# A delta-rule attention with a feed-forward: opening stage ordered by hand, weight decoding spread over VectorE, ACT and POOL beside the first feed-forwards, joins placed later

## The chip, the cores and the metric

The kernel runs on one core of a Trainium2 chip. The engines are TensorE (PE in the profile, PEld for its weight loads), VectorE (DVE), ScalarE (ACT), GpSimd (POOL) and SyncE (SP, which issues transfers). In these traces each of them works through its own instructions in the order as built, and one that has to wait holds up everything behind it: in the changed kernel VectorE stands 4.0 us behind one step of POOL, and a long transpose some steps further on starts at 175.9 us; without that kind of POOL step (run e2) it starts at 171.3.

## The reference, cut to what matters

```python
# attention: B=4, H=8, S=768, D=48; per head a 48 x 48 state
k_n = k / (norm(k, axis=-1) + 1e-6)
for t in range(S):
    y[t]  = q[t] @ state
    v_old = state^T k_n[t]
    state = state + beta[t] * outer(k_n[t], v[t] - v_old)
# feed-forward on x = y as (3072, 384); w_in 384 x 2048, w_out 2048 x 384, float64
out = gelu_exact(x @ w_in) @ w_out
```

Inputs are fp32 except the two weights. These arrive as 64-bit floats, which no step of the kernel reads as such: the kernel takes the two 32-bit words of each number and rebuilds an fp32 from mantissa, exponent and sign ("decoding").

## The kernel before

The sequence is cut into 12 chunks of 64 positions. For each pair of chunks (a "group") the loop over positions becomes a triangular system. Its parts are:

- *grams*: products of K and Q of a chunk (psG), packed into the tile `diag`;
- *flip*: VectorE transposes `diag` to `Nu`, so that all 32-row blocks are solved side by side;
- *elimination*: 30 pairs of dependent VectorE steps (`tmp`, then `Nu`), then three transposes back (`XM`, and `Zf` twice): the inverse;
- *joins*: TensorE joins the 32-row inverses to 64-row ones (psJ);
- *state steps*, chunk by chunk, because each needs the state of the one before: psK, W, psU, U, psY, x, psS, St, and psX/xT, x transposed for the feed-forward;
- *feed-forward* of a chunk: 16 times fc1 (psH) with a Gelu on ACT, then fc2 (psO).

Nothing of a feed-forward can start before the weights it needs are decoded, and nothing of chunk c's feed-forward before x of chunk c. The weights come in parts, each decoded by five VectorE steps and two POOL steps between them:

```python
def decode(n):
    ...
    nc.vector.tensor_scalar(e, hi, 20, 0x7FF, shift_right, and)          # exponent
    nc.vector.tensor_scalar(bits, hi, 0xFFFFF, 0x100000, and, or)        # high mantissa
    nc.gpsimd.tensor_scalar(e, e, 1151.0, 896.0, min, max)
    nc.gpsimd.tensor_scalar(e, e, -896.0, 2**23, add, mult)
    nc.vector.scalar_tensor_tensor(e, hi, 0x80000000, e, and, or)        # sign
    nc.vector.scalar_tensor_tensor(dst, lo, 2.0**-32, bits, mult, add)   # low mantissa
    nc.vector.scalar_tensor_tensor(dst, dst, 2.0**-20, e, mult, mult)
```

The order of the program is made by `interleave`, which spreads lists of steps over each other in proportion (a scheduler then still moves instructions within each engine):

```python
interleave(gram_steps(0) + gram_steps(1) + v_steps(0) + inverse_steps(0),
           [(1.0, decode, n) for n in range(6)])
interleave(state_steps(0), gram_steps(2) + v_steps(1),
           [(1.0, decode, n) for n in range(6, n_in)])
for c in range(1, NC):
    more = gram_steps(c + 2) + v_steps(c + 1) + (inverse_steps(c // 2 + 1) if c % 2 else [])
    ...  # c == 1: also the decode of w_out
    interleave(state_steps(c), more, ffn_steps(c - 1))
```

The norms of K take a power of one half on POOL (`nc.gpsimd.tensor_tensor(flat, flat, half, op=ALU.pow)`).

## Time and profile before

The kernel before took 827.5 us (median of 3 runs, 825.4 to 828.5). Its milestones, read from the timeline:

| milestone of the kernel before | us |
|---|---|
| first flip starts | 31.2 |
| first inverse (XM) ready | 102.0 |
| first fc1 | 126.5 |
| first feed-forward over | 213.0 |
| second feed-forward over | 267.6 |
| span | 825.5 |

How to read it: from 267.6 us on TensorE is busy for all but 14 of 558 us. Before that it is not, and what it waits for is VectorE.

### The profile page before, as it was taken

What the parts mean: (1) busy time and instruction counts of PE and PEld (TensorE: products, weight loads), DVE (VectorE), ACT (ScalarE), POOL (GpSimd) and SP (SyncE); (2) the same over time, 40 slices, a digit from 0 to 9 for tenths busy, and PEclk for the clock granted to TensorE, in tenths of its full rate; (3) what the DMA queues carried; (4) which work ended last, traced back from release to release, by engine and by line L of the source; (5) the groups of instructions that cost most, each with busy time, mean ns of one, the idle gap of its engine ahead of it and who ended that gap; (6) DMA issues with size and microseconds to landing.
All of it is one profiled execution on the core that took longest, in us unless ns stands there. A gap on an engine that the chain in (4) does not pass through costs nothing.

```text
span 825.5 us, 18581 instructions
## 1 busy us (share of the span) xinstructions
PE 707.5 (86%) x8148; PEld 515.3 (62%) x8148; DVE 376.1 (46%) x874; ACT 220.4 (27%) x510; POOL 190.9 (23%) x178
## 2 busy tenths in 40 slices
PE   4111078967999999999989999989999999999997
PEld 4100066735776865866857867757768668677684
DVE  3597997896012594031791023971125931202000
ACT  4200054201331512332403324213325122021120
POOL 8735357413002303013202014012023000000000
PEclk8555558887899999999999999999999999999999
DMA  7266034401101201203101102011011000000000
GB/s 173 111 154 107 19 90 106 102 33 30 35 16 29 50 1 30 40 12 61 19 20 31 30 21 54 6 30 31 2 30 30 2 21 2 10 11 1 20 1 19
DMA packets 84784, 32.85 MB, mean 40 GB/s; under 512 B 78048, under 2 KB 81120, under 8 KB 84704
## 3 DMA queue, kind: packets, MB, share of 16 engines
q1 hardware_dynamic: 80064, 26.75, 14.7%
q10 hardware_dynamic: 4640, 4.92, 2.4%
q8 instruction: 64, 1.05, 0.5%
q14 instruction: 16, 0.13, 0.0%
HBM read 26.94 MB, written 4.72 MB: 38 GB/s over the span
## 4 chain that ended last, share of the span: by engine, by line
PE 67%; DVE 20%; POOL 5%; issue 3%; SPq 2%; ACT 1%; DMA 1%; POOLq 0%; DVEq 0%
PE psO L460 28%; PE psH L451 25%; DVE tmp L283 4%; DVE Nu L285 4%; POOL w_e L187 2%; DVE w_e L189 2%; PE psT L235 2%; PE psS L426 2%; PE psG L248 2%; SPq L89 2%; PE psK L365 2%; PE psJ L320 1%; PE psJ L323 1%; DVE U L391 1%; PE psU L385 1%
## 5 line engine op out<-in xcount | busy, mean ns | idle before, releaser
L451 PE MATMUL psH<-xT,w_in_sb 128*128 128x256 f32 x1152 | 273.8, 390 | 4.0 <-ACT g L454 3.3
L460 PE MATMUL psO<-w_out_sb,g 128*128 128x384 f32 x768 | 273.6, 506 | 0.0
L451 PEld LDWEIGHTS psH<-xT,w_in_sb 128*128 128x128 f32 x1152 | 214.6, 192 | 36.4 <-ACT g L454 3.7
L460 PEld LDWEIGHTS psO<-w_out_sb,g 128*128 128x128 f32 x768 | 143.8, 194 | 91.0 <-issue 7.3
L454 ACT ACTIVATE g<-psH 128x256 f32<-128x256 f32 x192 | 73.7, 384 | 180.5 <-PE psH L451 179.9
L391 DVE TENSOR_TENSOR U<-psU,gm 64x192 f32<-64x192 f32 x88 | 31.2, 354 | 108.4 <-PE psU L385 107.5
L283 DVE TENSOR_TENSOR tmp<-Nu 128x30 f32<-128x30 f32 (+9 forms) x180 | 63.2, 351 | 4.6
L285 DVE TENSOR_TENSOR Nu<-Nu,tmp 128x30 f32<-128x30 f32 (+9 forms) x180 | 63.3, 352 | 4.4
L263 POOL TENSOR_TENSOR P<-G,mask 128x512 f32<-128x512 f32 x24 | 35.4, 1477 | 103.9 <-ACT G L253 103.9
L464 ACT COPY o_sb<-psO 128x384 f32<-128x384 f32 x24 | 11.5, 479 | 152.4 <-PE psO L460 152.4
L320 PE MATMUL psJ<-XM,off 32*32 32x32 f32 x768 | 16.4, 203 | 40.3 <-DVE XM L294 40.3
L235 PE MATMUL psT<-ident,Kp 128*128 128x128 f32 x96 | 17.0, 307 | 39.1 <-DMA Kp<-in_k_dram 29.1
L418 DVE TENSOR_TENSOR x<-psY,y 64x192 f32<-64x192 f32 x88 | 31.0, 352 | 38.4 <-PE psY L410 24.4
L320 PEld LDWEIGHTS psJ<-XM,off 32*32 32x32 f32 x768 | 15.2, 119 | 46.7 <-issue 43.4
L301 POOL MEMSET Zf<- 32x1024 f32 x12 | 11.4, 954 | 140.4 <-DVE Zf L298 140.1
L213 POOL TENSOR_TENSOR ksq<-Kp 128x384 f32<-128x384 f32 x24 | 20.7, 864 | 90.3 <-DMA Kp<-in_k_dram 90.0
L375 DVE TENSOR_TENSOR W<-psK,V 128x384 f32<-128x384 f32 x22 | 12.3, 557 | 61.9 <-PE psK L365 61.6
L187 POOL TENSOR_SCALAR w_e<-w_e 128x384 uint32<-128x384 uint32 (+1 forms) x28 | 27.4, 977 | 55.2 <-DVE w_e L183 54.9
L329 ACT COPY XM<-psJ 32x512 f32<-32x512 f32 x24 | 13.9, 578 | 97.7 <-PE psJ L320 97.6
L235 PEld LDWEIGHTS psT<-ident,Kp 128*128 128x128 f32 x96 | 12.7, 157 | 41.9 <-issue 35.9
L236 ACT COPY KQt<-psT 128x512 f32<-128x512 f32 x48 | 26.7, 588 | 43.6 <-PE psT L235 39.5
L214 DVE TENSOR_REDUCE n<-ksq 128x8 f32<-128x384 f32 x24 | 13.2, 552 | 55.2 <-POOL ksq L213 55.2
(75 smaller groups left out, 669.9 us busy)
## 6 DMA issues: line engine op xcount, KB each, us to landing
w_out_sb<-in_moe_w_in_dram SPq DMA_DIRECT2D x12, 512.0 KB, 4.7
w_raw<-in_moe_w_out_dram SPq DMA_DIRECT2D x16, 384.0 KB, 3.3
Kp<-in_k_dram SPq DMA_DIRECT2D x48, 96.0 KB, 2.9
Qp<-in_q_dram SPq DMA_DIRECT2D x48, 96.0 KB, 3.0
V<-in_v_dram SPq DMA_DIRECT2D x48, 96.0 KB, 2.9
out_dram<-o_sb ACTq DMA_DIRECT2D x48, 96.0 KB, 2.2
w_in_sb<-in_beta_dram ACTq DMA_DIRECT2D x2, 96.0 KB, 3.4
```

What stands on the lines that cost most here:

```text
L187: nc.gpsimd.tensor_scalar(e, e, 1151.0, 896.0, op0=ALU.min, op1=ALU.max)
L235: nc.tensor.transpose(psT[:, j, :], flat[:, j * 128:(j + 1) * 128], ident)
L236: nc.scalar.copy(u.KQt[:, :, :, x, :], psT.rearrange("q j (p n) -> q j p n", p=2))
L263: nc.gpsimd.tensor_tensor(u.P, G[:, :, C:], mask_h, op=ALU.mult)
L283: nc.vector.tensor_tensor(tmp, nu[:, j + 1:, j:j + 1].to_broadcast([128, n, j]), nu[:, j:j + 1, 0:j].to_broadcast([128, n, j]), op=ALU.mult)
L285: nc.vector.tensor_tensor(nu[:, j + 1:, 0:j], nu[:, j + 1:, 0:j], tmp, op=ALU.add)
L320: nc.tensor.matmul(psJ[low, 0, col], lhsT=off[top, u, :], rhs=xm[top, u, :], start=True, stop=True)
L391: nc.vector.tensor_tensor(pairs(u.U[HALF[p]], s), pairs(psU[HALF[p ^ s], p], s), pairs(gv[HALF[p]], s), op=ALU.mult)
L418: nc.vector.tensor_tensor(dst, src, pairs(u.y[HALF[p ^ s]], s), op=ALU.add)
L451: nc.tensor.matmul(psH, lhsT=w_in_sb[:, m, f * 128:(f + 1) * 128], rhs=xTs[c][:, m, :], start=(m == 0), stop=(m == NM - 1))
L454: nc.scalar.activation(gs[f], psH, ACT.Gelu)
L460: nc.tensor.matmul(u.psO, lhsT=gs[f][:, u.a * 128:(u.a + 1) * 128], rhs=w_out_sb[:, f, :], start=(f == 0), stop=(f == NF - 1))
```

## The change

The intent has five parts. (1) The opening is ordered by hand, free of most decode, with its own faster ways for square root and packing. (2) Only five half-width parts of the weights are decoded in the opening; 25 full parts go beside the first feed-forward, with the last steps of the small ones. (3) The decode drops from five VectorE steps to four; ACT takes two, POOL keeps one, the last product. (4) Everything after the opening is placed on a time line (`at(first, last, steps)`, in units of feed-forwards), with the joins behind the next chunk's first fc1. (5) K gets more tiles, so that it can be loaded earlier. The core of the diff, with cuts:

```diff
+        nc.vector.tensor_scalar(bits, hi, 0xFFFFF, 0x100000, op0=ALU.bitwise_and, op1=ALU.bitwise_or)
+        nc.scalar.mul(dst, bits, 2.0 ** -20)
         nc.vector.tensor_scalar(e, hi, 20, 0x7FF, op0=ALU.logical_shift_right, op1=ALU.bitwise_and)
-        nc.gpsimd.tensor_scalar(e, e, 1151.0, 896.0, op0=ALU.min, op1=ALU.max)
-        nc.gpsimd.tensor_scalar(e, e, -896.0, float(2 ** 23), op0=ALU.add, op1=ALU.mult)
+        nc.scalar.activation(e, e, ACT.Relu, bias=lim[:, 0:1], scale=float(2 ** 23))
+    def signed(n):
+        nc.vector.scalar_tensor_tensor(dst, lo, 2.0 ** -52, dst, ALU.mult, ALU.add)
         nc.vector.scalar_tensor_tensor(e, hi, 0x80000000, e, ALU.bitwise_and, ALU.bitwise_or)
-        nc.vector.scalar_tensor_tensor(dst, lo, 2.0 ** -32, bits, ALU.mult, ALU.add)
-        nc.vector.scalar_tensor_tensor(dst, dst, 2.0 ** -20, e.bitcast(F32), ALU.mult, ALU.mult)
+        nc.gpsimd.tensor_tensor(dst, dst, e.bitcast(F32), op=ALU.mult)
 ...
+    by_hand.enter_context(tc.manual_schedule(...))      # opening: grams, flip, elimination,
+    for fn, *args in rows:                              # joins of chunk 0, decode(0..4),
+        fn(*args)                                       # state of chunk 0, joins of chunk 1
 ...
+    plan = [at(c + 1, c + 2, ffn_steps(c)) for c in range(NC)]
+    plan += [at(1.0, 1.6, rest), ...]                   # rest: the other decode steps
+    plan += [..., at(1.6, 1.75, gram_steps(3)), at(1.75, 2.45, eliminate_steps(1)),
+             at(2.5, 2.62, join_steps(1)), at(2.62, 2.97, state_steps(2)), ...]
+    for w in range(3, NC):
+        plan += [at(w + 0.25, w + 0.95, state_steps(w))]
+        if w % 2:
+            plan += [at(w - 0.16, w - 0.15, [(1.0, prep, w + 2)]),
+                     at(w, w + 0.2, gram_steps(w + 2)),
+                     at(w + 0.2, w + 0.95, eliminate_steps(w // 2 + 1)),
+                     at(w + 1.02, w + 1.2, join_steps(w // 2 + 1))]
```

In the changed kernel the lines of the decode steps are L195, L197 (ACT), L198, L200 (ACT), L205, L206 and L207 (POOL's product); L252 is POOL's power, L333 the flip, L341 and L343 the elimination, L352 and L356 the transposes back, L378 and L381 the joins.

## The prediction

> **What bounds the kernel now.** I read the page's busy shares first, then the slices, then the busy-time windows cut at the feed-forwards' beginnings, then the timeline, tile and wait views of the stretches that stood out. The slices show two kernels in one:
>
> ```profile
> PE   4111078967999999999989999989999999999997
> DVE  3597997896012594031791023971125931202000
> PEclk8555558887899999999999999999999999999999
> ```
>
> TensorE is nearly idle for six slices of 20.6 us, half used for four more, then full. VectorE is the reverse. The cuts for the next view are the first fc1 matmul (126.5 us), the end of the first feed-forward (213.0) and of the second (267.6). Columns: stretch, length, busy us of PE, PEld, DVE, ACT, POOL, then granted clock.
>
> ```profile
> 0.00:126.50 126.50, 37.57 (x729) 31.48 (x729) 94.65 (x200) 29.82 (x62) 72.17 (x82) 0.56 0.46 110
> 126.50:213.00 86.50, 71.33 (x803) 50.30 (x800) 66.36 (x151) 20.07 (x45) 32.57 (x32) 0.83 0.24 60
> 213.00:267.60 54.60, 54.60 (x584) 39.71 (x577) 9.86 (x24) 16.91 (x40) 7.92 (x7) 1.00 0.15 30
> 267.60:825.50 557.90, 543.98 (x6048) 393.79 (x6046) 205.22 (x500) 153.63 (x364) 78.21 (x59) 0.99 0.11 22
> ```
>
> The last 558 us are TensorE-bound with 14 us of idle time; no rearrangement gains more than that there. The prize is the first 213 us, in which TensorE worked 109 us, much of it at half clock. The timeline says what it waited for: one VectorE chain from the first flip (L275) to the transposed-back inverse (L294), against the same chain for a later group, where no weights are decoded (in brackets: idle time before, and its releaser).
>
> ```profile
> 31.17 1.92 DVE L275 STREAM_TRANSPOSE Nu<-diag 128x1024 f32<-128x1024 f32 x1 [0.86 <-ACT diag L259]
> ...
> 100.01 2.00 DVE L294 STREAM_TRANSPOSE XM<-Nu 128x1024 f32<-128x1024 f32 x1
> ...
> 279.35 1.98 DVE L275 STREAM_TRANSPOSE Nu<-diag 128x1024 f32<-128x1024 f32 x1 [0.51 <-ACT diag L259]
> ...
> 308.02 2.08 DVE L294 STREAM_TRANSPOSE XM<-Nu 128x1024 f32<-128x1024 f32 x1
> ```
>
> The first takes 70.8 us, the later one 30.7 us, of which 2.9 are two interleaved U groups: 27.8 us alone. So 43 us of the opening is weight decoding threaded into the elimination, whose VectorE steps wait for POOL steps in between:
>
> ```profile
> L187 POOL TENSOR_SCALAR w_e<-w_e x28: 507/686/2253, 33.5 to 172.5; 128x384 uint32<-128x384 uint32 x16, 128x512 uint32<-128x512 uint32 x12
> L183 DVE TENSOR_SCALAR w_e<-w_raw x16: 319/352/565, 96.1 to 172.1; 128x384 uint32<-128x384 uint32 x16
> L189 DVE SCALAR_TENSOR_TENSOR w_e<-w_raw,w_e x16: 508/559/1618, 98.2 to 174.0; 128x384 uint32<-128x384 uint32 x16
> L183 DVE TENSOR_SCALAR w_e<-w_out_sb x12: 394/415/1044, 33.0 to 91.8; 128x512 uint32<-128x512 uint32 x12
> L189 DVE SCALAR_TENSOR_TENSOR w_e<-w_out_sb,w_e x12: 676/680/1305, 35.8 to 94.5; 128x512 uint32<-128x512 uint32 x12
> ```
>
> The three numbers are least, median and greatest ns.
>
> **What the Trainium skill says.** "VectorE: DVE Perf Modes", section on the perf-mode tier table: fp32 work with one tensor source reaches twice the rate, with two sources the single rate. The trace agrees: 415 ns against 680 ns at 512 columns. "GPSIMD Engine Reference", Specifications: GpSimd's SBUF interfaces are shared with VectorE, contended by two-port modes and by two SBUF inputs. The trace agrees: the one POOL form L187 ranges from 507 to 2253 ns. "ScalarE: Activation LUTs", What ACT_TABLE_LOAD costs: a load is about 1283 ns, an ACTIVATE 186 ns plus 0.833 ns per element, 93 ns more with a pointer bias. The trace shows both loads at 1283 ns and a 256-column SBUF copy at 405 ns (the formula gives 399). "TensorE: Matmul & The Clock Gate", Part 1: the array runs at half rate after idling and recovers after a few us of work. The PEclk row shows 5 throughout the opening.
>
> **The change part by part.** (1) *Opening to the flip.* K goes out on two issuers; in the timeline an issue takes 0.66 us and landing 2.9, so K is in at about 6.5 us, and the last Q, fourteenth on its queue, is issued at about 10 and in at 13. The square root moves from POOL (2.9 us each) to eleven small VectorE operations of about 0.2 us. ACT has eight KQt copies (0.59) and six G copies (0.54): 8 us, and TensorE eight transposes of 0.6 to 1.1 us and four grams of 1 to 2 us. From the last Q: transpose, KQt copy, gram, G copies, packing, about 8 us with handovers, and 2 us for queueing behind the others. Flip at about 23 us, before 31.2.
>
> (2) *The elimination alone*: 27.8 us. Inverse ready at 23 + 28 = 51 us, before 102.
>
> (3) *To the first fc1.* Before, 24.5 us from there (102 to 126.5). The changed order puts only chunk 0's joins ahead. On the path: two Zf transposes 3.7, decode steps between them 0.5, POOL memsets 2.0, solve 2.2 at half clock, U 2.9, read 1.1, x copies twice 1.3, transposes and xT copies 2.5: about 17 us. First fc1 at 68 us instead of 126.5: **58 us gained** so far.
>
> (4) *What this puts off.* Only five of 31 parts (half-width ones) are decoded by then; before, twelve full parts of w_in and some of w_out were. Nine parts of 512 and sixteen of 384 remain beside the first feed-forward. Each costs VectorE two one-source and two two-source steps; with an overlap of about 0.08 us a step, the medians make 1.95 us (512) and 1.5 us (384). 9 x 1.95 + 16 x 1.5 = 41.6 us; I add 15% for POOL, which keeps one two-input product a part, and 2 us for the small parts left: 50 us. The stretch also holds VectorE's own state and gram work (W, U, x, St, off, two norms): 13.5 us by the group means. So VectorE needs 63 us and finishes decoding at about 131; handovers through ACT (25 parts of about 1.1 us by the skill's formula beside its 25 us of copies and Gelus, so ACT is nearly full) add some 2: 133 us. TensorE needs about 60 us in this stretch (41.6 for a feed-forward, as the last one shows, plus state and two grams), so VectorE is the bound, narrowly. In the order as built, POOL has XM, P and other work ahead of the last product: some 5 us, then 5 us of last fc2 matmuls. First feed-forward over at about 143, before 213.
>
> (5) *Second feed-forward.* The second elimination may start only after the decode, at about 139; its inverse is ready at 139 + 28 = 167. TensorE has 21 us of fc1 with nothing else placed in it, 143 to 164, then waits about 3 us at the first join. Then 20.8 us of fc2 and about 14 of state, gram and joins, with 2 of waits: over at about 204, before 267.6. **Gain 63.6 us.**
>
> (6) *The steady part.* Matmul counts are unchanged. Before, each pair of chunks lost about 2.3 us, the clock being 0.97 in some:
>
> ```profile
> 267.60:330.80 63.20, 60.80 (x817) 43.84 (x815) 40.66 (x99) 19.13 (x44) 14.76 (x11) 0.97 0.14 27
> 330.80:385.30 54.50, 54.50 (x576) 39.65 (x575) 9.86 (x24) 16.91 (x40) 7.80 (x7) 1.00 0.15 30
> PE psS L426 <- DVE x L418: 9.0, 4, 2.4
> ```
>
> The nine us is a state product waiting for a PSUM buffer that x frees, and x stands behind the inverse's transposes. In the new order the first x comes before them, and the joins fall after the next chunk's first fc1. I count 6 of those 9 us and 2 us of clock. The homes for K remove DMA-queue waits that TensorE does not see: nothing by themselves. 557.9 - 8 = 550.
>
> Sum: 204 + 550 = 754 us of span; the time before exceeds its span by 2, so **756 us**, a ratio of 0.914.
>
> **The rivals.** *A: ACT or POOL becomes the bound beside the first feed-forward.* ACT would be over 80% full and works in order: a Gelu that waits for TensorE holds up the decode's scaling, and VectorE then idles. For it: the 2253 ns maximum above, and that VectorE waited 10.4 us for POOL's w_e steps before. Against it: the decode runs one part ahead of its second half. If it holds, decoding ends near 150 and the time is 770 to 776. *B: the fixed order of the opening is worse than counted*: every engine there runs in order, so one late Q or slow POOL packing delays the flip. Each us is paid in full; 5 to 8 us, hence 761 to 764. *C: little gain, because the decode is only moved.* Then fc1 begins early but starves, and the first feed-forward ends where it did, at 213 or a little earlier: about 820. Against it: VectorE was idle 32 of the first 126 us and 20 of the next 86, partly waiting for POOL; and 29 us of elimination leave the decode's stretch. *D: all goes better*: uncontended decode and no wait at the first join: 745.
>
> **Range and chances.** The three uncertain terms are the opening (plus or minus 5), the decode stretch (minus 6, plus 12) and the steady part (plus or minus 5). Combined, with the longer tail upwards: 743 to 774. Only something like C with trouble besides would miss 2%: faster 0.97, same 0.02, slower 0.01.
>
> **What would show it.** In the changed profile the first flip should start near 23 us, its inverse be back at about 51, the first fc1 at 68, the last decode step at 133, and the first two feed-forwards end near 143 and 204. VectorE should be over 85% busy from 68 to 133 with TensorE visibly idle there; if ACT is busier than VectorE, or VectorE's idle time there ends on ACT or POOL, rival A holds. A flip after 30 us shows B. The psS wait should fall to 3 us or less, the stretch from the third feed-forward on to about 550. I am wrong if the first fc1 comes after 80 us or the steady part lengthens.

## More of the kernel before

The metric is the device time of one execution in microseconds (us), as the median of several runs; all runs told of here were classed as fast, none as disturbed.

One more line is of use later, the page's first part (busy us, share of the span, number of instructions):

```profile
PE 707.5 (86%) x8148; PEld 515.3 (62%) x8148; DVE 376.1 (46%) x874; ACT 220.4 (27%) x510; POOL 190.9 (23%) x178
```

## The result, and the profile after

The changed kernel took **813.86 us** (median of 4 runs, 813.58 to 814.46), the kernel before 827.95 us. The ratio is 0.9837, 95% interval 0.9815 to 0.9858: a gain of 1.6%, within the 2% that counts as the same. Ratios here are the mean time of one kernel's fast runs over that of the other's in the same rounds, so not quite the ratio of the medians. The prediction was 756 us.

The page's first part, after:

```profile
PE 704.0 (87%) x8148; PEld 509.4 (63%) x8148; DVE 383.6 (47%) x869; ACT 245.4 (30%) x561; POOL 173.6 (21%) x161
```

Here is the first warning: the change took one step of five from every decoded part on VectorE, yet VectorE is busy 7.5 us *longer* than before (383.6 against 376.1). The slices of the span, now 20.3 us each:

```profile
PE   5116687795599989999989999989999989999997
...
DVE  4896799867531792132980132960215940301100
...
PEclk9655879998699999999999999999999999999999
```

TensorE is at six tenths or more from the fourth slice on, where before it was from the sixth. But a dent has come in slices 10 and 11 (the two fives), after the first feed-forward, at 183 to 223 us. Cut at the milestones, the stretches look like this (stretch, length, busy us of PE, PEld, DVE, ACT, POOL with instruction counts, granted clock, DMA share, GB/s):

```profile
0.00:27.20 27.20, 13.74 (x172) 11.01 (x172) 13.27 (x36) 10.25 (x19) 14.63 (x32) 0.98 0.75 138
27.20:56.60 29.40, 0.00 (x0) 0.00 (x0) 27.24 (x65) 0.00 (x0) 5.96 (x6) 0.50 0.44 94
56.60:82.90 26.30, 17.98 (x462) 15.90 (x463) 17.12 (x36) 12.22 (x29) 9.90 (x12) 0.50 0.45 109
82.90:167.00 84.10, 64.48 (x627) 44.11 (x626) 78.27 (x137) 46.06 (x97) 48.75 (x39) 0.87 0.41 113
167.00:175.90 8.90, 7.91 (x28) 4.69 (x27) 4.80 (x8) 3.74 (x9) 8.53 (x10) 1.00 0.49 100
175.90:211.10 35.20, 18.27 (x84) 15.74 (x84) 28.05 (x77) 5.64 (x15) 7.47 (x4) 0.80 0.04 9
211.10:252.70 41.60, 39.94 (x726) 27.19 (x727) 13.07 (x24) 13.66 (x29) 8.46 (x7) 0.93 0.18 35
252.70:812.10 559.40, 541.73 (x6055) 390.73 (x6053) 201.81 (x491) 153.84 (x365) 69.88 (x54) 1.00 0.10 20
```

The cuts are: first flip, first inverse, first fc1, last decode step on VectorE, second flip, second inverse, end of the second feed-forward. Read the DVE column: 27 of 29, then 78 of 84, then 28 of 35. VectorE sets the time from the first flip to the second inverse, with one gap between 56.6 and 82.9. The two inverses, from the timeline:

```profile
27.23 1.94 DVE L333 STREAM_TRANSPOSE Nu<-diag 128x1024 f32<-128x1024 f32 x1
54.57 2.02 DVE L352 STREAM_TRANSPOSE XM<-Nu 128x1024 f32<-128x1024 f32 x1
...
175.88 1.95 DVE L333 STREAM_TRANSPOSE Nu<-diag 128x1024 f32<-128x1024 f32 x1
...
209.04 2.00 DVE L352 STREAM_TRANSPOSE XM<-Nu 128x1024 f32<-128x1024 f32 x1
```

The prediction's sum can be laid beside these cuts term by term. This is the whole miss:

| term | predicted us | measured us | difference |
|---|---|---|---|
| start to first flip | 23 | 27.2 | +4.2 |
| first elimination | 28 | 29.4 | +1.4 |
| inverse to first fc1 | 17 | 26.3 | +9.3 |
| first fc1 to last decode step | 65 | 84.1 | +19.1 |
| to the second flip | 6 | 8.9 | +2.9 |
| second elimination | 28 | 35.2 | +7.2 |
| inverse to end of second feed-forward | 37 | 41.6 | +4.6 |
| all the rest | 550 | 559.4 | +9.4 |
| span | 754 | 812.1 | +58.1 |

Against the kernel before, the first fc1 came 43.6 us earlier (82.9 for 126.5). Of that, 40.4 us were left at the end of the first feed-forward (172.6 for 213.0), 14.9 at the end of the second (252.7 for 267.6) and 13.4 at the end of the span.

**The longest term.** The decode steps on VectorE in the changed kernel, from the views of their lines between 83 and 172 us (least, median, greatest ns; first and last start; form):

```profile
L205 DVE SCALAR_TENSOR_TENSOR w_in_sb<-w_out_sb,w_in_sb x10: 420/950/1755, 87.4 to 116.5; 128x512 f32<-128x512 uint32 x9, 128x256 f32<-128x256 uint32 x1
L205 DVE SCALAR_TENSOR_TENSOR w_out_sb<-Zf,w_out_sb x8: 552/1352/1627, 119.3 to 157.8; 128x384 f32<-128x384 uint32 x8
...
L207 POOL TENSOR_TENSOR w_out_sb<-w_out_sb,w_e x16: 994/1046/1248, 121.7 to 168.0; 128x384 f32<-128x384 f32 x16
```

One and the same step takes from 552 to 1627 ns. The timeline, with POOL beside VectorE, shows when it is long:

```profile
119.16 1.33 POOL L207 TENSOR_TENSOR w_in_sb<-w_in_sb,w_e 128x512 f32<-128x512 f32 x1 [1.50 <-DVE w_e L206]
119.28 1.63 DVE L205 SCALAR_TENSOR_TENSOR w_out_sb<-Zf,w_out_sb 128x384 f32<-128x384 uint32 x1
120.83 0.35 DVE L198 TENSOR_SCALAR w_e<-Zf 128x384 uint32<-128x384 uint32 x1
121.10 0.55 DVE L206 SCALAR_TENSOR_TENSOR w_e<-Zf,w_e 128x384 uint32<-128x384 uint32 x1
...
121.72 1.05 POOL L207 TENSOR_TENSOR w_out_sb<-w_out_sb,w_e 128x384 f32<-128x384 f32 x1 [1.23 <-DVE w_e L206]
121.83 1.35 DVE L205 SCALAR_TENSOR_TENSOR w_out_sb<-Zf,w_out_sb 128x384 f32<-128x384 uint32 x1
```

POOL's product starts at 119.16 and ends at 120.49; the VectorE step that starts 0.12 us after it ends at 120.91, 0.42 us after the product. In the next pair: 122.77 and 123.18, 0.41 us after. So the VectorE step does not run slower beside the product, it stands until the product is over and then does its work. With POOL quiet (L206 at 121.10) a two-input step of this size takes 0.55 us.

The step of one input is held up too, and so is a step beside other work of POOL (here the mask of the elimination, `XM`):

```profile
106.58 1.39 POOL L207 TENSOR_TENSOR w_in_sb<-w_in_sb,w_e 128x512 f32<-128x512 f32 x1 [1.57 <-DVE w_e L206]
106.76 1.49 DVE L195 TENSOR_SCALAR w_in_sb<-w_out_sb 128x512 uint32<-128x512 uint32 x1
...
163.88 2.67 POOL L328 TENSOR_TENSOR XM<-low,gt 128x1024 f32<-128x1024 f32 x1
164.26 2.70 DVE L206 SCALAR_TENSOR_TENSOR w_e<-w_raw,w_e 128x384 uint32<-128x384 uint32 x1
```

The first of these ends 0.28 us after POOL's step, the second 0.41 us. All 102 decode steps of VectorE between 82.9 and 167 us took 72.8 us (13.9, 13.0, 27.4 and 18.5 for L195, L198, L205 and L206); at their shortest they would have taken 49.0 us (9 parts of 512 columns at 2 x 0.414 + 2 x 0.680, 16 of 384 at 2 x 0.346 + 2 x 0.545, and 0.8 for two steps of the half part). Read one by one in the timeline, 27 steps make up nearly all of the 23.8 us between. Twenty of them, 5 with one input and 15 with two, stood behind POOL's product: 17.2 us. Seven stood behind POOL's other steps (`V`, `ksq`, `P`, `XM`): 6.3 us.

The Trainium skill describes just this: "SBUF — State Buffer", section "SBUF: two separate sides", says that VectorE and GpSimd have one port pair in common, which is an exclusive lock and not a division of bandwidth; a VectorE step that runs in a two-port mode or has two SBUF inputs, and a GpSimd step that reads SBUF, block each other, and the one that started first keeps the pair for the whole instruction. The trace agrees, with the 0.41 and 0.42 us above and with the held steps of one input. The prediction cited another page, which says only that there is contention, and put 15% for it.

**The waits.** From the waits view of TensorE (70 to 222 us) and that of VectorE (82.9 to 211 us): us in all, times, longest.

```profile
PE psJ L378 <- DVE XM L352: 17.0, 1, 17.0
PE psH L504 <- ACT g L507: 11.0, 7, 4.5
```

```profile
DVE n L231 <- POOL n L252: 16.8, 5, 4.6
```

TensorE stands 17.0 us before the first join of the second group. VectorE stands 16.8 us behind POOL's power: the norms of five chunks, 2 to 6, are in its stream by then, drawn ahead by the scheduler, and at each of them the stream stands.

**The rest.** The chain of waits of the changed kernel where chunk 3's state meets the third group's inverse (start, us, what):

```profile
298.71 0.04 DVE XM L352
298.75 1.93 issue
300.68 1.89 DVE Zf L356
302.57 0.17 DVE x L470
302.75 0.36 DVE x L470
303.12 0.36 DVE x L470
303.50 0.36 DVE x L470
303.86 0.14 issue
303.99 0.68 PE psS L478 x32
```

The x that TensorE needs to go on stands behind two transposes of the inverse, 3.9 us from 298.71 to 302.57. It was so before; the changed order did not mend it. The wait of psS for x from the third feed-forward on is 11.1 us in eight places, where the prediction's 9.0 were to fall to 3.

### The profile page after: what moved, and what is told of

The parts are those of the page before. It is cut to its first block, busy times and chain, and to the rows that moved or that the text cites. A ratio compares the mean times of both kernels' runs of the same rounds, so it can differ in the third digit from the quotient of the medians.

```text
span 812.1 us, 18594 instructions
## 1 busy us (share of the span) xinstructions
PE 704.0 (87%) x8148; PEld 509.4 (63%) x8148; DVE 383.6 (47%) x869; ACT 245.4 (30%) x561; POOL 173.6 (21%) x161
## 3 DMA queue, kind: packets, MB, share of 16 engines
q1 hardware_dynamic: 79184, 26.55, 14.9%
q8 instruction: 64, 1.05, 0.5%
## 4 chain that ended last, share of the span: by engine, by line
PE 57%; DVE 31%; issue 4%; POOL 3%; DMA 2%; ACT 2%; SPq 0%; ACTq 0%; POOLq 0%; DVEq 0%
PE psO L513 21%; PE psH L504 21%; DVE Nu L343 8%; DVE tmp L341 8%; PE psT L279 2%; PE psG L287 2%; DVE U L443 2%; DVE x L470 2%; PE psJ L381 2%; DVE w_e L206 2%; PE psJ L378 1%; DVE w_out_sb L205 1%; POOL n L252 1%; DVE w_in_sb L205 1%; DVE w_e L198 1%
## 5 line engine op out<-in xcount | busy, mean ns | idle before, releaser
L504 PE MATMUL psH<-xT,w_in_sb 128*128 128x256 f32 x1152 | 277.5, 391 | 13.3 <-ACT g L507 11.0
L341 DVE TENSOR_TENSOR tmp<-Nu 128x30 f32<-128x30 f32 (+9 forms) x180 | 63.1, 351 | 5.7
L343 DVE TENSOR_TENSOR Nu<-Nu,tmp 128x30 f32<-128x30 f32 (+9 forms) x180 | 63.1, 351 | 5.4
L378 PE MATMUL psJ<-XM,off 32*32 32x32 f32 x768 | 16.6, 203 | 50.7 <-DVE XM L352 50.3
L314 POOL TENSOR_TENSOR P<-G,mask 128x512 f32<-128x512 f32 x22 | 32.7, 1488 | 126.5 <-ACT G L294 126.5
L517 ACT COPY o_sb<-psO 128x384 f32<-128x384 f32 x24 | 11.5, 479 | 135.8 <-PE psO L513 133.5
L378 PEld LDWEIGHTS psJ<-XM,off 32*32 32x32 f32 x768 | 15.2, 118 | 54.6 <-issue 54.1
L359 POOL MEMSET Zf<- 32x1024 f32 x12 | 11.5, 956 | 152.9 <-DVE Zf L356 125.1
L269 POOL TENSOR_TENSOR V<-V,n 128x384 f32<-128x384 f32 x24 | 21.7, 908 | 77.5 <-DMA V<-in_v_dram 68.0
L310 DVE TENSOR_TENSOR off<-G,gm 128x256 f32<-128x256 f32 x20 | 12.9, 647 | 51.6 <-ACT G L294 51.6
L491 ACT COPY xT<-psX 128x384 f32<-128x384 f32 x24 | 11.3, 477 | 80.6 <-PE psX L490 80.6
L294 ACT COPY G<-psG 128x512 f32<-128x512 f32 x44 | 23.6, 587 | 37.5 <-PE psG L287 34.0
L387 ACT COPY XM<-psJ 32x512 f32<-32x512 f32 x24 | 13.9, 578 | 63.3 <-DVE w_e L198 33.0
L252 POOL TENSOR_TENSOR n<-n,half 128x16 f32<-128x16 f32 x10 | 29.3, 2932 | 12.4 <-DVE n L241 11.7
```

Of the source, the lines that this page charges most:

```text
L294: copy(G[:, :, r, :], psG[:, r])
L314: nc.gpsimd.tensor_tensor(u.P, u.G[:, :, C:], mask_h, op=ALU.mult)
L341: nc.vector.tensor_tensor(tmp, nu[:, j + 1:, j:j + 1].to_broadcast([128, n, j]), nu[:, j:j + 1, 0:j].to_broadcast([128, n, j]), op=ALU.mult)
L343: nc.vector.tensor_tensor(nu[:, j + 1:, 0:j], nu[:, j + 1:, 0:j], tmp, op=ALU.add)
L378: nc.tensor.matmul(psJ[low, 0, col], lhsT=off[top, u, :], rhs=xm[top, u, :], start=True, stop=True)
L504: nc.tensor.matmul(psH, lhsT=w_in_sb[:, m, f * 128:(f + 1) * 128], rhs=xTs[c][:, m, :], start=(m == 0), stop=(m == NM - 1))
```

## The experiments

The theory after reading: VectorE's in-order stream sets the time from the opening to the second inverse. It is longer than counted because POOL's two-input product locks it out, and because it stands behind POOL's power. The steady part lost its gain to the place of x. Rivals: ACT or TensorE's order sets the end of the first feed-forward; VectorE is simply full by the number of its steps; the elimination is hidden. Sixteen kernels ran. The kernel before spreads over 6 us (for example 822.0 to 828.3), the kernels over 0.2 to 3.5 us, so I compare these by their medians with the changed kernel's 813.9 us, and check with milestones in the traces. The changed kernel was not run again beside the experiments, which ran on chips 12, 14 and 3; the medians of the kernel before lay between 822.7 and 828.0 us, so a difference of a microsecond or two to 813.9 us is not resolved. "Second" is the start of the last output copy of the second feed-forward; it is 252.9 us in the changed kernel.

| kernel | median us | ratio to before, 95% interval | second |
|---|---|---|---|
| changed | 813.9 | 0.984 (0.982 to 0.986) | 252.9 |
| e1_product_vector | 804.6 | 0.976 (0.973 to 0.980) | 244.1 |
| e5_no_product (wrong result) | 793.8 | 0.964 (0.960 to 0.967) | 233.6 |
| e3_half_elim | 803.4 | 0.975 (0.971 to 0.979) | 242.2 |
| e4_join1_later | 814.3 | 0.988 (0.984 to 0.992) | 252.6 |
| e2_no_pow | 804.2 | 0.973 (0.970 to 0.976) | 244.1 |
| e7_product_no_pow | 791.8 | 0.959 (0.955 to 0.963) | 229.1 |
| e8_early_second | 791.6 | 0.958 (0.954 to 0.963) | 231.1 |
| e6_steady_order | 802.3 | 0.972 (0.968 to 0.975) | 252.6 |
| e9_all | 780.3 | 0.945 (0.942 to 0.949) | 230.8 |
| e10_fuller_opening | 781.6 | 0.946 (0.943 to 0.949) | 231.9 |
| e12_fuller_serial | 780.2 | 0.945 (0.942 to 0.947) | 230.7 |
| e11_old_decode | 815.2 | 0.986 (0.983 to 0.990) | 255.5 |
| e13_half_first | 803.9 | 0.975 (0.972 to 0.977) | 242.1 |
| e16_fc2_ahead_alone | 808.3 | 0.980 (0.978 to 0.983) | 246.2 |
| e14_fc2_ahead | 776.3 | 0.941 (0.938 to 0.944) | 225.0 |
| e15_late_prep | 776.7 | 0.942 (0.939 to 0.944) | 225.4 |

### The decode's product: e1, e5, e11

```diff
 # e1_product_vector
-        nc.gpsimd.tensor_tensor(dst, dst, e.bitcast(F32), op=ALU.mult)
+        nc.vector.tensor_tensor(dst, dst, e.bitcast(F32), op=ALU.mult)
```

> Edit: the decode's last product (weight times signed power of two) goes from POOL to VectorE; nothing else changes. Contention theory: the decode steps of VectorE beside the first feed-forward took 72.5 us in the changed kernel where their shortest durations (two one-input steps of 0.346 and two two-input steps of 0.545 us for 384 columns, 0.414 and 0.680 us for 512) sum to 48 us, and the 24 us are what POOL's product takes from VectorE. With the product on VectorE and POOL silent, five undisturbed steps are 2.33 us (384) and 2.87 us (512), 63 us in all: one step more for each part and yet some 9 us less. First feed-forward shorter by 6 to 10 us, the whole by 5 to 10 us: 804 to 809 us; the two-input step L205 back at 0.55 and 0.68 us. Rival, count: VectorE is bound by the number of its steps and the stretch has another source (transfers landing in its tiles), so 25 more steps add 14 us: 826 to 830 us. Rival, not bound: the end of the first feed-forward hangs on TensorE or ACT, and the time stays within 3 us of 814.

804.6 us: 9.3 us less, although VectorE was given a step *more* for each part. Its lines in the same views:

```profile
L205 DVE SCALAR_TENSOR_TENSOR w_in_sb<-w_out_sb,w_in_sb x10: 415/676/679, 86.5 to 114.3; 128x512 f32<-128x512 uint32 x9, 128x256 f32<-128x256 uint32 x1
L205 DVE SCALAR_TENSOR_TENSOR w_out_sb<-Zf,w_out_sb x8: 539/550/1159, 116.6 to 155.8; 128x384 f32<-128x384 uint32 x8
```

The medians are back at the shortest durations of the changed kernel: 676 ns for 950, 550 for 1352. The four old steps together take 51.2 us in place of 72.8, and what is still stretched (2.1 us) stands behind POOL's other steps. Transfers into VectorE's tiles, which were the rival's source of the stretch, are as many as before.

```diff
 # e5_no_product: the result is wrong on purpose
-        nc.gpsimd.tensor_tensor(dst, dst, e.bitcast(F32), op=ALU.mult)
```

> Edit: the decode's last product is left out altogether (the result is wrong on purpose; the other steps and their order stay). Contention theory: VectorE's decode steps fall from 72.5 us to near their floor of 48 us, the first feed-forward from 89.7 us to 68 to 75 us (then TensorE, 69 us busy there, or VectorE's 13 us of attention beside 48 us of decode, sets it), and the whole to 795 to 802 us, where the wait for the second inverse keeps it. Rival, not bound: steps shorten, the time stays within 3 us of 814. Rival, count or transfers: steps keep their lengths, time within 3 us of 814.

793.8 us, 20.1 us less than the changed kernel, and the first feed-forward's last output copy starts at 153.0 us in place of 173.7. That is what the theory said, for the total as for the first feed-forward (20.7 us less). The wait before the second joins stayed, 17.8 us, which fits: the second elimination starts after the decode and moved with it. In e1 and e5 VectorE's waits behind the power did not shrink (18.3 and 20.6 us up to 211 us, 16.8 in the changed kernel), so the gain is not theirs.

```diff
 # e11_old_decode
-        nc.scalar.mul(dst, bits, 2.0 ** -20)
-        nc.scalar.activation(e, e, ACT.Relu, bias=lim[:, 0:1], scale=float(2 ** 23))
+        nc.gpsimd.tensor_scalar(e, e, 1151.0, 896.0, op0=ALU.min, op1=ALU.max)
+        nc.gpsimd.tensor_scalar(e, e, -896.0, float(2 ** 23), op0=ALU.add, op1=ALU.mult)
-        nc.vector.scalar_tensor_tensor(dst, lo, 2.0 ** -52, dst, ALU.mult, ALU.add)
+        nc.vector.scalar_tensor_tensor(dst, lo, 2.0 ** -32, dst.bitcast(U32), ALU.mult, ALU.add)
-        nc.gpsimd.tensor_tensor(dst, dst, e.bitcast(F32), op=ALU.mult)
+        nc.vector.scalar_tensor_tensor(dst, dst, 2.0 ** -20, e.bitcast(F32), ALU.mult, ALU.mult)
```

> Edit: the changed kernel with the arithmetic of the decode of before (five steps on VectorE, two one-input steps on POOL, none on ACT), in the same places; this undoes one part of the change alone. Theory: the new split takes one step of five from VectorE but stretches the others: before, the five steps took 3.09 us (384 columns) and 3.18 us (512), 78 us for the 25 parts beside the first feed-forward, against 72.5 us now; so the split is worth only 3 to 8 us: 817 to 822 us. The prediction's step (decode 50 us in the new form) would have it worth some 28 us: 838 to 842 us. A third: the new split is a loss, 805 to 812 us.

815.2 us. The new split of the decode, in the same places, is worth 1.3 us against the old one, which is too little to tell from nothing here. That is below even the theory's 3 to 8 us, and far from the 28 us that the prediction's step implies. Four VectorE steps of which some stand behind a product cost about as much as five beside POOL's one-input steps.

### VectorE behind POOL's power: e2, e7

```diff
 # e2_no_pow; e7_product_no_pow is this on top of e1
-        flat = n.rearrange("q a h -> q (a h)")
-        nc.gpsimd.tensor_tensor(flat, flat, half, op=ALU.pow)
+        root(n)          # eleven small VectorE steps, as in the opening
```

> Edit, on top of e1_product_vector: every square root of the norms is taken by VectorE's eleven small steps (some 2.2 us) and not by POOL's power (2.9 us, with VectorE standing still for 2.8 to 4.0 us each time). Theory: VectorE's stream sets the second inverse; it stood 16.8 us behind POOL's power five times up to 211 us, and pays about 11 us for the roots in their place, so the joins of the second group come 5 to 7 us earlier and the whole is 797 to 801 us (e1: 804.6). Rival: the power waits lie beside other waits of the same elimination (the grams from ACT), and nothing is gained: 803 to 806 us.

791.8 us, 12.8 us less than e1 and more than expected. The second flip came at 161.9 us, where it was 169.3 in e1, the transpose of the inverse at 190.1 for 202.8, and the wait before the joins fell from 15.7 us to

```profile
PE psJ L377 <- DVE XM L351: 7.8, 1, 7.8
```

> Edit, alone on the changed kernel: the square roots of the norms by VectorE's eleven small steps in place of POOL's power; the decode's product stays on POOL. Theory: e7 gained 12.8 us over e1 by this, more than the 4 to 8 expected, 7.5 us of it before the second elimination's flip; the waits are there in the changed kernel too (16.8 us in five waits up to 211 us), so 801 to 806 us. Rival: with POOL's product in place VectorE is stretched anyway and the roots gain little: 810 to 814 us.

804.2 us, 9.6 us less than the changed kernel, as the theory had it. So with the product left on POOL, moving the power gains as much as moving the product did. VectorE spends more busy time on eleven small steps than it would on none; but a step that it does itself is not one it stands behind.

### The second inverse and TensorE's order: e3, e8, e16

```diff
 # e3_half_elim (wrong by the letter of the algorithm)
-        steps += [(0.7, eliminate, j) for j in range(1, HB - 1)]
+        steps += [(0.7, eliminate, j) for j in range(1, HB - 1) if g != 1 or j % 2]
```

> Edit: the second elimination (chunks 2 and 3) skips every second row (15 of 30; result wrong on purpose), all else stays. The elimination of 28 us becomes some 13 us shorter. Theory: the 17.0 us that TensorE stood before the first join of the second group, waiting for the inverse from VectorE, are on the path, so the second feed-forward ends 11 to 14 us earlier: 800 to 803 us. Rival, hidden: the wait falls but what follows (state of chunk 2 behind decode, clock, chunk 4) sets the end; gain under 4 us: 810 to 814 us.

803.4 us, 10.5 us less; the theory's 11 to 14 us were slightly too much, the rival's under 4 are out. The result passes the comparison all the same: the rows left out matter less than its tolerance. The wait of psJ fell to

```profile
PE psJ L378 <- DVE XM L352: 6.1, 1, 6.1
```

that is by 10.9 us, and the end moved by as much. So that wait is on the path.

```diff
 # e8_early_second, on top of e7
-             at(1.12, 1.6, state_steps(1)), at(1.5, 1.51, [(1.0, prep, 3)]),
-             at(1.6, 1.75, gram_steps(3)), at(1.75, 2.45, eliminate_steps(1)),
-             at(2.5, 2.62, join_steps(1)), at(2.62, 2.97, state_steps(2)),
+             at(1.12, 1.6, state_steps(1)), at(1.3, 1.31, [(1.0, prep, 3)]),
+             at(1.35, 1.5, gram_steps(3)), at(1.5, 2.2, eliminate_steps(1)),
+             at(2.28, 2.4, join_steps(1)), at(2.42, 2.97, state_steps(2)),
```

> Edit, on top of e7_product_no_pow: chunk 3's norms, grams and the second elimination begin before the last parts are decoded (0.2 to 0.25 of a feed-forward earlier in the plan), the joins and the state of chunk 2 likewise, as in the kernel before, where the second elimination ran beside the first feed-forward. Theory (VectorE's total work from the first fc1 to the second inverse is the bound, order matters only where it stands idle): first feed-forward ends 10 to 25 us later, the wait before the second joins disappears, and the second feed-forward ends 0 to 6 us earlier: 793 to 800 us. Rival: the serial order was the fault, and beside decode the elimination is hidden: 780 to 788 us.

791.6 us, the same as e7. The wait before the joins fell to 3.5 us, the end of the first feed-forward went from 159.1 to 165.2 us: with elimination and decode side by side the time only moves between the two feed-forwards. The rival (serial order was the fault) is out.

```diff
 # e16_fc2_ahead_alone
-             at(2.5, 2.62, join_steps(1)), at(2.62, 2.97, state_steps(2)),
+             at(2.62, 2.72, join_steps(1)), at(2.72, 3.0, state_steps(2)),
```

> Edit, alone on the changed kernel: the joins of the second group are planned at 2.62 to 2.72 in place of 2.5 to 2.62 and the state of chunk 2 behind them, which puts 8 of the 32 second-product matmuls of the second feed-forward ahead of the joins. Theory: they fill 5 us of the 17 us wait, and the end of that feed-forward comes 3 to 6 us earlier: 808 to 811 us. Rival: what follows the joins is a chain of short products that needs those matmuls beside it, and the time is lost again there: 813 to 816 us.

808.3 us, 5.5 us less. TensorE does 5 us of fc2 in the time in which it stood before; the wait is 11.8 us. The hole was thus due to VectorE's late inverse *and* to TensorE's order, which had the joins ahead of all fc2 work.

### The opening: e4, e13

```diff
 # e4_join1_later
-    for level in range(2):
-        join(0, 1, level)
+    plan += [at(1.04, 1.1, join_steps(0, (1,)))]
```

> Edit: the joins of chunk 1 leave the hand-ordered opening and come 4 to 10 per cent into the first feed-forward. Theory: they hold TensorE and ACT for some 5 us ahead of the first fc1, so the first fc1 comes 4 to 6 us earlier (77 to 79 us against 82.9), but beside the first feed-forward VectorE's decode is the bound and is not moved, so the end of that feed-forward moves by 0 to 3 us and the whole is 811 to 814 us. Rival, path is TensorE's order: the gain of 4 to 6 us goes through to the end: 808 to 810 us.

The first fc1 came at 77.5 us in place of 83.1, and the time stayed at 814.3 us. The 5.6 us that chunk 1's joins hold up TensorE, which the prediction had overlooked, cost nothing. The end of the first feed-forward even moved 3.9 us back (177.6 for 173.7), more than the theory's 0 to 3, and that too left no trace at the end of the second (252.6).

```diff
 # e13_half_first (wrong by the letter of the algorithm)
-        steps += [(0.7, eliminate, j) for j in range(1, HB - 1)]
+        steps += [(0.7, eliminate, j) for j in range(1, HB - 1) if g or j % 2]
```

> Edit, alone on the changed kernel: the first elimination (chunks 0 and 1) skips every second row, so the opening's VectorE chain is some 13 us shorter (by the letter of the algorithm the result is wrong on purpose; it may lie within the tolerance, as it did for the second). Theory: the opening reaches the end through VectorE's stream (opening, decode, second elimination), so that the first fc1 comes at 70 us and the whole falls by 8 to 13 us: 801 to 806 us. Rival: the opening is covered by something else (the fetch of the weights, or POOL), as it looked in e4: 810 to 815 us.

803.9 us: 9.9 us less. The inverse came 10.9 us earlier, and the second flip as much (timeline of e13):

```profile
27.26 1.94 DVE L333 STREAM_TRANSPOSE Nu<-diag 128x1024 f32<-128x1024 f32 x1
43.63 2.01 DVE L352 STREAM_TRANSPOSE XM<-Nu 128x1024 f32<-128x1024 f32 x1
...
164.98 1.95 DVE L333 STREAM_TRANSPOSE Nu<-diag 128x1024 f32<-128x1024 f32 x1
```

54.57 to 43.63 at the first inverse, 175.88 to 164.98 at the second flip: VectorE's stream hands the whole 10.9 us of the opening on, and 9.9 of them reach the end. Together with e4 this tells the two apart: the opening counts through VectorE, not through the first fc1.

### The steady part: e6

```diff
 # e6_steady_order
-        plan += [at(w + 0.25, w + 0.95, state_steps(w))]
+        plan += [at(w + 0.22, w + 0.82, state_steps(w))]
-                     at(w + 0.2, w + 0.95, eliminate_steps(w // 2 + 1)),
-                     at(w + 1.02, w + 1.2, join_steps(w // 2 + 1))]
+                     at(w + 0.22, w + 1.02, eliminate_steps(w // 2 + 1)),
+                     at(w + 1.06, w + 1.2, join_steps(w // 2 + 1))]
```

> Edit, alone: from the third feed-forward on, the state steps of each odd chunk end earlier (0.82 in place of 0.95 of their feed-forward) and the elimination runs a little past its end (1.02), so that both x come before the transposes that carry the inverse back. Theory: the changed kernel's plan still put x behind them (the chain of waits has psS after x after 3.8 us of transposes), so the 11 us that TensorE waits for x from the third feed-forward on fall to 3 us or less, and the time by 6 to 9 us: 805 to 808 us. Rival: what is gained there is lost again in front of the joins, since the inverse comes later: 812 to 816 us.

802.3 us: 11.6 us less, more than the theory's 6 to 9. The first 253 us are as in the changed kernel; the gain is in the rest, whose window reads

```profile
253.10:800.50 547.40, 540.30 (x6052) 390.19 (x6050) 201.62 (x491) 152.78 (x365) 69.99 (x54) 1.00 0.10 21
```

547.4 us with 7.1 idle for TensorE, against 559.4 with 17.7. No wait of psS for x is listed in that stretch any more.

### Together: e9, e10, e12, e14, e15

e9 is e8 and e6 together.

> Edit: e8_early_second and e6_steady_order together. Theory: their gains lie in different stretches and add: 786 to 793 us. Rival: 795 us or more.

780.3 us, 33.6 us less than the changed kernel. The parts add: 22.1 (e7, to which e8 added nothing) and 11.6 (e6) make 33.7.

e10 puts four more parts of the decode into the opening; e12 is the same with the second elimination behind the decode again:

```diff
 # e10_fuller_opening on top of e9, e12 on top of e7 and e6; cut
+    for i, u in enumerate(first[:NA]):
+        read(u)
+        decode(3 + i)
+        turn(u)
+        signed(3 + i)
+    decode(5)
+    decode(6)
 ...
-    rest = decode_steps(5, NW)
+    rest = decode_steps(9, NW)
```

> Edit, on top of e9_all: the hand-ordered opening decodes nine parts (0 to 8) in place of five, their VectorE steps put where VectorE stood for PE and ACT between the first inverse and the first fc1 (9.8 us of those 27 us in e9_all). Theory: beside the first feed-forward VectorE is the bound (busy 80.7 of 81.7 us in e9_all), so 11 us of decode taken out of it and put mostly into idle time make it 4 to 8 us shorter: 772 to 777 us. Rival: ACT's share of the four parts holds up x and the first fc1 by as much: 779 to 783 us.

> Edit: e10_fuller_opening with the second elimination after the decode again, as in the changed kernel. Theory: e7 and e8 gave the same time, because the sum of VectorE's work is what counts and not its order; so within 3 us of e10. Rival: with the steady part mended and the opening filled the order does count: over 4 us apart.

781.6 and 780.2 us: no gain over e9, so the theory's 4 to 8 us did not come, though the two agree with each other as expected. The first half of the theory did come true. In e12 VectorE is busy 24.1 of the 27 us from 56 to 83, where it was 17.5 in e9, and the second inverse starts on its way back at 186.5 us, 3.6 us earlier than in e7, which has the same order of elimination and decode. The end did not follow, and TensorE's timeline of e12 shows where the 3.6 us went:

```profile
188.62 1.92 PE L377 MATMUL psJ<-XM,off 32*32 32x32 f32 x64 [11.52 <-DVE XM L351]
190.47 5.25 PE L512 MATMUL psO<-w_out_sb,g 128*128 128x384 f32 x8
...
197.74 2.85 PE L512 MATMUL psO<-w_out_sb,g 128*128 128x384 f32 x8
```

In the order as built, all fc2 products of the second feed-forward stand behind the first join; in e7 sixteen of them (5.3 us) came ahead of it. So TensorE stood 11.5 us in place of 7.8, had the same work left after it, and did its first eight products in 5.25 us, which later take 2.85. The gain had become a wait.

e14 puts e16's order on e12, and e15 besides loads and takes the norms of chunks 4 to 6 later:

> Edit: the same on top of e12_fuller_serial (780.2 us), where TensorE waits 11.5 us for the second inverse. Theory: half of that wait is filled, 774 to 777 us. Rival: 779 to 782 us.

> Edit: e14_fc2_ahead with the norms of chunks 4 and 5 (two sets of eleven small steps, with their sums, some 8 us of VectorE) loaded and taken later, so that the second inverse no longer stands behind them. Theory: the inverse comes 5 to 8 us earlier and the time falls by 3 to 6 us more: 769 to 774 us. Rival: the scheduler puts them, or something else, in the same place: within 2 us of e14.

776.3 us for e14, 3.9 less than e12, as expected: the wait is 6.2 us. That the gain of the fuller opening now comes out is not shown: the same order gave 5.5 us by itself (e16), and no run has it on top of e7 and e6 without the fuller opening. e15 gave 776.7 us, as its rival said. The trace tells why: three sets of roots lie between the second flip (160.4) and the way back of the inverse (188.7), as in e14. The scheduler had put them back, so what they cost is not shown by this run. The traces allow an estimate, though: from the second flip to the start of the way back, roots included, e14 takes 28.3 us (158.79 to 187.08). The first elimination of the changed kernel, which has no roots in it, takes 27.3 us, some 2 us of it in three steps held up at its start. So the roots cost that stretch some 1 to 3 us, less than the 5 to 8 us hoped for.

**e14 is the best kernel**: 776.3 us, ratio 0.941 to the kernel before, a correct result, and no new idea: it is the changed kernel with its last product and its roots on VectorE, the decode of four more parts in the opening and three shifts of order.

## Why the prediction was wrong

By its own steps:

- **What bounds the kernel**: right, and it held in the changed kernel. VectorE set the first part, TensorE the rest.
- **Step 1, flip at 23**: 27.2. A term mis-sized by 4.2 us. No run took it apart. The trace of the changed kernel shows TensorE standing 5.2 us for the first Q, up to 10.64 us, with the transposes of the other K behind it in its stream, while the transpose of the last Q, at 20.56 us, waits for no transfer: so the sum that starts from the last Q's arrival starts from the wrong one. Whether another order would bring the 4.2 us back is open. e13 shows that a microsecond of this kind on VectorE's stream costs about one at the end.
- **Step 2, elimination alone 28**: right, 29.4.
- **Step 3, 17 us to the first fc1**: 26.3. "The changed order puts only chunk 0's joins ahead" was false: chunk 1's joins and a transpose also stood ahead. e4 shows that this error cost nothing, because the first fc1 was not what the first feed-forward waited for. "58 us gained so far" counted as a gain what was not on the path.
- **Step 4, decode 50 us of VectorE**: this is the step that failed. "I add 15% for POOL, which keeps one two-input product a part". The 41.6 us before the addition were about right (four steps of 512 columns, 2.19 us, less 0.32 us make 1.87 us and not 1.95, a slip of 0.7 us in all): 49.0 us of undisturbed durations, each step overlapping the next by 0.08 us as L198 at 120.83 does, make 41 us. The addition was wrong in kind and in size. POOL does not slow VectorE by a share, it locks it out for what is left of its own step: 17.2 us behind the product, 35% and not 15% of the 49.0 us, and 6.3 us behind POOL's other steps, which were not counted at all. e1 and e5 show it: one more step on VectorE is 9 us faster, no product at all 20 us. In the same term, VectorE's 7.4 us behind the power (two waits) were not counted; 2 us were, for ACT. Yet the kernel before has 14.2 us of such waits in its first 213 us; its waits view has them beside the 10.4 us that rival A quotes. ACT was not the trouble: it was busy 46 of those 84 us, and **rival A** held only in that VectorE's waits there ended on POOL.
- **Step 5, the second elimination**: 6 us to the flip became 8.9, and 28 us of elimination 35.2. The plan put nothing else there, but the scheduler drew the norms of chunks 4 to 6 into VectorE's stream, with 4.0 us behind the power just ahead of the flip, and 2.6 and 2.8 us within the elimination. e2 took these waits and the two earlier ones away, for 9.6 us. The 3 us wait at the first join became 17.0; e3 took 10.9 of them away and the time fell by 10.5, so that they are on the path.
- **Step 6, "in the new order the first x comes before them"**: false for the order as built; the chain of waits shows x behind the transposes. The mechanism was right, and the size too small: when x does come first, 11.6 us go (e6), where 8 were claimed.
- **Two readings of the lines** were loose: the slices before show TensorE nearly idle for five slices, not six, and then at six to nine tenths, not half; and the granted clock is 0.8 in the first slice, 0.5 only in the next five. The window view below them is read rightly, and no term of the sum hangs on this.
- **Its signs of being wrong** both came: the first fc1 after 80 us (82.9) and a longer steady part (559.4 us for 557.9). By e4 the first of them was harmless; the sign that mattered was the last decode step, 167 for 133.
- **Rival C**, "the decode is only moved", put at about 820 us, came nearest, for the reason it gave: fc1 begins early and starves. What spoke against it in the prediction was VectorE's idle time before, and that 29 us of elimination leave the decode's stretch. But VectorE's busy time rose by 7.5 us, the time in held-up steps included, and the elimination that left the stretch came behind it, on the path.

Where the opening's 43.6 us went can now be said: 3.2 in the first feed-forward, starved by a stretched decode, 25.5 in the second, behind an elimination that before ran beside the first, and 1.5 in the rest. Repairs of the causes shown (e9) gave 33.6 us back, 37.6 with the fuller opening and the order of fc2 (e14); of the 58 us missed, some 20 remain. I count 4.2 of them to the flip. The rest has built up by the last decode step: in e14 the inverse is ready at 56.5 us, the first fc1 comes at 86.5 and the last decode step ends at 153.4, where 51, 68 and 133 were predicted. VectorE is still full there: in e12 it is busy 74.2 of the 75 us from 83 to 158, and 29.1 of the 30 us from there to the inverse. Its stream then has a fifth step for each part and eleven small ones for each root; no run settles how much of that could still go elsewhere. The load of K on two issuers and its further tiles were not tried by themselves.

## What to carry to other kernels

Before giving an engine's step to another, ask what the two have in common: here a two-input product on GpSimd held up VectorE's steps, of two inputs and of one, until it was over (17.2 us in 20 steps), so on a path set by VectorE the step that "offloads" can cost more than it takes away. Count the work by the in-order stream that sets the end: an earlier start of TensorE was worth nothing while VectorE's stream was the same (e4), and a microsecond taken from that stream was worth about one (e3, e5, e13), unless TensorE's order turned it into a wait (e12). When a stage is moved from beside another to behind it, check in the instruction order as built what was drawn into it, and what that waits for.

## What the Trainium skill lacked or had wrong

- "GPSIMD Engine Reference", Specifications, names contention between GpSimd and VectorE steps with two SBUF inputs or in a two-port mode, without its size; read alone it led to 15%. "SBUF — State Buffer", "SBUF: two separate sides", has the rule (an exclusive lock for the whole instruction), and the runs agree with it: a VectorE step of 0.55 us took 1.35 to 1.63 us beside products of 1.05 to 1.33 us, and ended 0.41 to 0.42 us after them.
- No page that I found has the cost of a power on GpSimd: the ten of 128 x 16 elements took 2.93 us on the average, where eleven VectorE steps, mostly of 0.12 to 0.25 us, do the same work (e14).
- No page that I found says what the exchange of a lock-bound step is worth: e1 had 25 more VectorE steps and was 9.3 us faster.
